# A retention and mixture-of-experts kernel: slot sums in 32-by-32 pieces, phi's products summed in PSUM, out-state in 64-by-64 pieces, phi's loads ahead of routing

## The chip, the cores and the metric

The kernel runs on one core of a Trainium2 chip. The metric is the device time of one execution in microseconds (us). The kernel before was run three times: median 550.13 us, from 546.73 to 552.35. One more execution was profiled; it took 551.17 us, of which the profile's span covers 549.3.

## The reference

Three layers follow one another. All data are float32. The first is a gated retention over 4 batches, 8 heads, 768 steps and head size 64, with a running 64-by-64 state per head:

```python
for t in range(S):
    state = gamma * state + einsum('bhd,bhe->bhde', k[:, :, t], v[:, :, t])
    y[:, :, t] = scale * einsum('bhd,bhde->bhe', q[:, :, t], state)
```

Its output, 3072 tokens of 512 numbers, goes through a top-1 mixture of 8 experts (512 to 1024 to 512, each token through the expert that its gate picks), scaled by the gate's softmax and a sigmoid. The third layer is a soft mixture over 32 slots: `logits = x @ phi`; a softmax over the tokens makes each slot's input `d.T @ x`; 8 more experts act on 4 slots each; a softmax over the slots sends the result back to the tokens:

```python
logits = x @ phi
d = softmax over tokens of logits
slot_input = d.T @ x
slot_out[e] = relu(slot_input[e] @ w1[e]) @ w2[e]
out = softmax over slots of logits @ slot_out
```

## The kernel before, in words

The order of the work is written out by hand on every engine. There are three parts.

**The loop (lines 525 to 552).** 24 tiles of 128 tokens, and two more rounds for what lags. A round follows the table ORDER, whose names are functions: `s0` scores of k with q (line 359, eight products of 64-row halves); `oq` out-state (line 384: four 128-by-128 products of the scaled q with a block-diagonal copy `bds` of the states of two heads, half of it zeros); `os` out-scores (394); `st` the state's update (406, needs `k_scale`'s product of GpSimd, line 342); `xt` transposes (446); gate products and the rank of each token in its expert (427, 439, 493, 494). `pl` (line 508) has GpSimd send the 128 tokens' numbers to their places in a list `inv` in DRAM by an indirect transfer. Those transfers write one tensor, so each waits until the one before has landed, the last one excepted. SyncE's queue issues the loads of tile i+3 (`kt`, `qt`, `vn`, `kn`, 256 KB each), the store `xs` of a finished tile (256 KB), and one load `wt` (512 KB) for phi.

That `wt` load is a quarter of one expert's second weight matrix, transposed. The logits need x times phi where x is h times w2, so the kernel prepares `wps`, w2 times phi, for each expert: `wq_mm` (line 290) multiplies a quarter by phi in four column groups, one for each 128 rows of the contracted axis; ScalarE copies the four partial results (293); `wq_sum` (303) adds them with a product by a selection matrix; ScalarE copies again (307) and after four quarters stores the expert's `wps` (309). There are 32 such units, one for a round of the loop from the fourth on; nine are left behind the loop, and the last five loads (two of them issued before the order is known, three after the first lists) with them.

**Routing (lines 555 to 700).** A product counts the tokens of each expert (`cp`, line 556), VectorE ranks the experts by count, and SyncE and ScalarE read the rank. Then the first weights are loaded (line 191), the first expert's list of tokens (`xidx`, 575, on ScalarE's queue, after the last transfers into `inv`), and a branch is passed on every engine that is taken only when an expert has more tokens than planned. Then GpSimd gathers the tokens' rows (`xg`, 723).

**The experts (lines 890 to 960), then the tail.** For each of 8 experts 8 steps f: TensorE computes `hps` (758) as three products in the rounded float format, ScalarE and VectorE split the weights (200, 201), and beside that `behind(e - 1, f)` does a part of the expert before. At f 2 and 3 the exponentials of the logits are transposed by VectorE into `pd` (823, four 32-row bands), a block-diagonal 128-by-128 matrix for each block of 32 tokens; at f 4 `slot_h` (866) multiplies each of 14, 13 or 12 blocks by the block's `hB` (256 columns), all in one accumulation; at f 5 VectorE transposes the sum (872); at f 6 and 7 `slot_in` (878) multiplies by w2. The tail computes the slots' experts from 128 loads `m` (256 KB each, 52 of them and more prefetched) and writes the output.

## Time and profile before

| what | value |
|---|---|
| median of three runs | 550.13 us |
| the profiled execution | 551.17 us, span 549.3 us |
| TensorE products / weight loads busy | 490.8 us (89%) / 360.2 us (66%) |
| VectorE, ScalarE, GpSimd busy | 266.0, 187.8, 124.5 us |
| read from HBM, written | 118.64 MB, 14.17 MB |

TensorE is busy nearly all the time, but a float32 product shows as two records (two passes), records of different parts of the array overlap, and a record's end is modelled. So the share alone does not tell how much a stage could give; the stages are read one by one. Times in the rows are microseconds from the start of the span.

### The profile page before, as it was taken

To read this page: it belongs to the slowest core of one execution; us is meant where nothing else is said; L and a number is where in the kernel's file an instruction comes from. 1 tells how busy PE (TensorE), PEld (TensorE's weight loads), DVE (VectorE), ACT (ScalarE), POOL (GpSimd) and SP (SyncE) were. 2 spreads that over 40 slices of the span, in tenths; PEclk is the share of its full clock that TensorE was granted. 3 is DMA by queue.
4 is the path that set the end of the run, shared out by engine and by line. 5 is a ranking of instruction groups with operands and counts; after the bars stand their busy time and mean duration, and the time that the engine had idled before them with its cause. 6 is when DMAs were issued, how large, how long until landed. Compare 5 with 4: busy or idle time off the path is not lost.

```text
span 549.3 us, 11022 instructions
## 1 busy us (share of the span) xinstructions
PE 490.8 (89%) x3869; PEld 360.2 (66%) x3869; DVE 266.0 (48%) x820; ACT 187.8 (34%) x486; POOL 124.5 (23%) x130
## 2 busy tenths in 40 slices
PE   4998889997998569999999899999999896789993
PEld 3876667775875348887786877858588582534152
DVE  1756545643663004574554846556475553234032
ACT  1453434452453115442433424233352331013042
POOL 2313222223322112131506023060411103020020
PEclk9999979996996559999999999999999999799997
DMA  8999796979567835782947829387493716999858
GB/s 263 356 335 359 219 340 204 336 237 310 177 207 238 196 114 164 229 260 80 341 153 250 276 73 362 108 297 233 139 333 97 245 58 220 369 388 380 325 184 276
DMA packets 77489, 133.63 MB, mean 243 GB/s; under 512 B 14226, under 2 KB 23056, under 8 KB 77424
## 3 DMA queue, kind: packets, MB, share of 16 engines
q1 hardware_dynamic: 68640, 120.79, 67.0%
q0 software_dynamic: 4176, 8.41, 4.5%
q10 hardware_dynamic: 4608, 3.63, 2.0%
q8 instruction: 33, 0.54, 0.5%
q14 instruction: 32, 0.26, 0.1%
HBM read 118.64 MB, written 14.17 MB: 242 GB/s over the span
## 4 chain that ended last, share of the span: by engine, by line
PE 47%; DMA 6%; DVE 4%; issue 2%; ACT 2%; POOL 1%; SPq 1%; ACTq 1%; POOLq 0%
PE hps L758 19%; PE gps L866 9%; PE slo L878 4%; PE so L1047 4%; PE xps L731 3%; PE fh L1008 3%; DMA w<-in_moe_w_dram 2%; PE lps L789 2%; DVE pd L823 2%; DMA r<-in_moe_w_dram 2%; DMA m<-in_moe_w_dram 1%; PE ops L1105 1%; PE warm L748 1%; ACT ot L1107 1%; POOL xg L723 1%
## 5 line engine op out<-in xcount | busy, mean ns | idle before, releaser
L758 PE MATMUL hps<-xh,wh 128*128 128x416 f32 (+2 forms) x256 | 94.2, 368 | 0.0
L758 PE MATMUL hps<-xh,wl 128*128 128x416 f32 (+2 forms) x256 | 88.8, 347 | 0.0
L758 PE MATMUL hps<-xl,wh 128*128 128x416 f32 (+2 forms) x256 | 88.7, 346 | 0.0
L763 ACT ACTIVATE h<-hps 128x416 f32<-128x416 f32 (+2 forms) x64 | 32.6, 510 | 122.9 <-PE hps L758 112.2
L201 DVE TENSOR_TENSOR wl<-r,wh 128x512 fp32r<-128x512 f32 x64 | 43.6, 682 | 58.8 <-ACT wh L200 57.8
L853 POOL DMA_INDIRECT ctok<-cn,xidx x29 | 28.8, 995 | 185.3 <-DVE cn L850 178.9
L758 PEld LDWEIGHTS hps<-xh,wh 128*128 128x128 f32 x256 | 48.0, 188 | 17.8 <-issue 15.9
L369 DVE TENSOR_TENSOR sS<-s,csa 128x512 f32<-128x512 f32 x48 | 30.9, 685 | 51.8 <-PE s L359 34.5
L866 PE MATMUL gps<-hB,pd 128*128 128x256 f32 x204 | 49.0, 400 | 7.7 <-DVE pd L823 7.4
L866 PEld LDWEIGHTS gps<-hB,pd 128*128 128x128 f32 x204 | 40.1, 200 | 16.2 <-issue 5.8
L758 PEld LDWEIGHTS hps<-xl,wh 128*128 128x128 f32 x256 | 48.1, 188 | 1.6 <-issue 0.8
L508 POOL DMA_INDIRECT inv<-tok,pos x24 | 24.8, 1031 | 106.4 <-DMA inv<-tok,pos 22.4
L758 PEld LDWEIGHTS hps<-xh,wl 128*128 128x128 f32 x256 | 48.1, 188 | 0.8 <-DVE wl L201 0.2
L200 ACT ACTIVATE wh<-r 128x512 fp32r<-128x512 f32 x64 | 40.0, 626 | 15.8 <-DMA r<-in_moe_w_dram 9.6
L723 POOL DMA_INDIRECT xg<-xs,xidx x29 | 29.4, 1015 | 55.9 <-PE xps L731 32.2
L303 PEld LDWEIGHTS wsum<-cs,wr 128*128 128x128 f32 x128 | 22.3, 248 | 22.8 <-issue 10.6
L359 PE MATMUL s<-qt,kt 64*128 64x128 f32 x384 | 31.6, 308 | 5.1 <-DMA qt<-in_qt_dram 5.1
L878 PE MATMUL slo<-w,gt 128*32 128x512 f32 x128 | 30.4, 604 | 4.8 <-DMA w<-in_moe_w_dram 2.2
L770 DVE STREAM_TRANSPOSE hB<-h 128x416 f32<-128x416 f32 (+2 forms) x64 | 34.5, 578 | 0.0
L740 DVE TENSOR_TENSOR xl<-xps,xh 128x416 fp32r<-128x416 f32 (+2 forms) x32 | 18.4, 583 | 28.8 <-issue 20.5
L359 PEld LDWEIGHTS s<-qt,kt 64*128 64x128 f32 x384 | 26.4, 208 | 7.0 <-DMA kt<-in_kt_dram 5.3
L394 PE MATMUL o<-sS,vn 128*64 128x128 f32 x384 | 28.3, 285 | 2.5 <-DVE sS L369 2.5
(144 smaller groups left out, 716.1 us busy)
## 6 DMA issues: line engine op xcount, KB each, us to landing
m<-in_moe_w_dram SPq DMA_DIRECT2D x128, 256.0 KB
wt<-in_moe_w_dram SPq DMA_DIRECT2D x32, 512.0 KB
r<-in_moe_w_dram SPq DMA_DIRECT2D x64, 256.0 KB
w<-in_moe_w_dram SPq DMA_DIRECT2D x64, 256.0 KB
vn<-in_vn_dram SPq DMA_DIRECT2D x24, 256.0 KB
xs<-xnat SPq DMA_DIRECT2D x24, 256.0 KB
kt<-in_kt_dram SPq DMA_DIRECT2D x23, 256.0 KB
qt<-in_qt_dram SPq DMA_DIRECT2D x23, 256.0 KB
```

The lines of the kernel that those rows point to most:

```text
L200: nc.scalar.activation(out=hi, in_=t, func=ACTF.Copy)
L201: nc.vector.tensor_tensor(out=lo, in0=t, in1=hi, op=ALU.subtract)
L359: nc.tensor.matmul(out=ps[h][:, p, :], lhsT=raw["kt", i][r, p, :], rhs=raw["qt", i][r, p, :], start=True, stop=True, tile_position=(64 * h ...
L369: nc.vector.tensor_tensor(out=sS[i][:, :, h, :], in0=sps.pop((i, h)), in1=con("dm", 128).rearrange("p (a b) t -> p a b t", b=2)[:, :, h, : ...
L394: nc.tensor.matmul(out=o[64 * h:64 * h + 64, p, :], lhsT=vv[:, 2 * p + h, :], rhs=s[:, p, h, :], start=(c == 0 and p == 0), stop=True, ski ...
L723: nc.gpsimd.indirect_dma_start(out=xg[e][j][0:r, :], out_offset=None, in_=xs[:, :], in_offset=bass.IndirectOffsetOnAxis(ap=xidx[e][0:r, j: ...
L758: nc.tensor.matmul(out=ps, lhsT=a[:, kk * 128:(kk + 1) * 128], rhs=x[e][kk][:, 0:c], start=(n == 0), stop=(n == 11))
L763: nc.scalar.activation(out=hs[g][:, 0:c], in_=ps, func=ACTF.Relu)
L770: nc.vector.transpose(out=hB[e][:, 0:NB[e], f, :], in_=hs[e * KF + f][:, 0:c].rearrange("p (b t) -> p b t", t=32))
L853: put = nc.gpsimd.indirect_dma_start(out=ctok[:, :], out_offset=bass.IndirectOffsetOnAxis(ap=xidx[e][0:r, j:j + 1], axis=0), in_=cn[0:r, j ...
L866: nc.tensor.matmul(out=ps, lhsT=pd[:, b, :], rhs=hB[e][:, b].rearrange("p f t -> p (f t)"), start=(b == 0), stop=(b == NB[e] - 1))
L878: nc.tensor.matmul(out=slo[e][32 * i:32 * i + 32, :], lhsT=gts[e][:, hf * 4 + i, :], rhs=w2n[e, hf][i], start=(hf == 0), stop=(hf == 1), s ...
```

## The change

Four edits, and the rearrangements that they need.

1. **Slot sums.** `pd` with its zeros is gone; one VectorE transpose over all 128 partitions makes `pT_`. `slot_h` issues, for each block of 32 tokens and each of four 32-row bands, one product of 32 rows by 32 columns (4 times as many products as before, each over 256 columns). The band decides the array's rows and the PSUM bank, the block modulo 4 the array's columns. `slot_c` copies the four banks (two on ScalarE, two on VectorE), and `slot_t` adds the column groups by eight products with the selection matrix.
2. **phi's products.** `wq(e)` takes a whole expert: 16 products, the four column groups each a quarter of the result, accumulated over the contracted axis in PSUM. There is no `wsum` and no copy to it; one VectorE transpose gives the layout that is stored. It runs in rounds 5, 8, ..., 23 of the loop, and once behind it.
3. **Out-state.** Eight products of 64 by 64 in the four quarters of the array; `bds` holds no zeros and is copied by one instruction in place of two. To keep each head in its quarter the order of the heads in x changes, which the host mirrors in the weights' rows.
4. **Loads ahead of routing.** `wt` is loaded at four thirds of a load per round, in contiguous 512 KB, 10 buffers in place of 6; all 32 loads are issued inside the loop. An indirect transfer into `inv` waits for the third before it instead of the one before. The first list `xidx` moves from ScalarE's queue to SyncE's, and the second weight load moves ahead of the later reads of the rank. In ORDER, `st` moves ahead of `os`.

```diff
-ORDER = ("s0 xe sc m0 g1 rm m1 oq gc g2 G0 ne G2 os G3 st G1 G4 G6 rk G7 G8 G9 zk pl G10 "
-         "G5 zq xt G11").split()
+WAT = {5 + 3 * e: e for e in range(E)}
+ORDER = ("s0 xe sc m0 g1 rm m1 oq gc ne g2 G0 G2 wp st os G3 G1 G4 G6 rk G7 G8 G9 zk pl G10 G5 zq xt G11").split()
-PB = dict(s=3, o=1, g=2)
+PB = dict(s=2, o=1, g=2)
...
+        def wq_load(e, kk):
+            if e < E:
+                wtt[e, kk] = wst.tile([128, FF], F32, tag="wt", name="wt")
+                nc.sync.dma_start(out=wtt[e, kk], in_=moe_w2[1, e, kk * 32:(kk + 1) * 32, :].rearrange("a (b f) -> (a b) f", f=FF))
+        def wq(e):
+            ps = pT.tile([128, 512], F32, tag="xn", name="wps")
             for kk in range(KD):
-                nc.tensor.matmul(out=ps[32 * kk:32 * kk + 32, 0:256], lhsT=phi[:, kk, :], rhs=t[:, kk, :],
-                                 start=True, stop=True, skip_group_check=True)
...
+                t = wtt.pop((e, kk))
+                for g in range(4):
+                    nc.tensor.matmul(out=ps[32 * g:32 * g + 32, 0:256], lhsT=phi[:, kk, :], rhs=t[:, 256 * g:256 * g + 256],
+                                     start=(kk == 0), stop=(kk == KD - 1), skip_group_check=True)
+            ws = sc2.tile([128, KF, NS], F32, tag="ws", name="ws")
+            nc.vector.transpose(out=ws, in_=ps[:, 0:256].rearrange("p (b t) -> p b t", t=32))
+            nc.scalar.dma_start(out=wps[e].rearrange("p (f s) -> p f s", s=NS), in_=ws)
...
-                    nc.tensor.matmul(out=o[:, p, :], lhsT=bds[(i - 1) % 2][:, p, :], rhs=q2[i][:, p, :],
-                                     start=(p == 0), stop=False, skip_group_check=True)
+                    for h in range(2):
+                        r = slice(64 * h, 64 * h + 64)
+                        nc.tensor.matmul(out=o_at(i, p, h), lhsT=bds[(i - 1) % 2][r, p, :], rhs=q2[i][r, p, :],
+                                         start=(p < 2), stop=False, tile_position=(64 * h, 64 * (h ^ p % 2)), skip_group_check=True)
...
-            for h in range(2):
-                r = slice(64 * h, 64 * h + 64)
-                nc.scalar.copy(out=bds[i % 2][r, :, r], in_=stp[0][r])
+            nc.scalar.copy(out=bds[i % 2], in_=stp[0])
...
-            if i == NTILE - 1:
-                tc.declare_no_dep(put.ins, places[-1].ins, reason="tokens have distinct slots")
-                after(put, places[-2:-1])
+            for prev in places[-2:]:
+                tc.declare_no_dep(put.ins, prev.ins, reason="tokens have distinct slots")
+            after(put, places[-3:-2])
...
-            wq_load(i + 1)
-            wq_mm(i - WLAG)
-            wq_sum(i - WLAG - 1)
+            for u in range(max(0, (i - 1) * 4 // 3), max(0, i * 4 // 3)):
+                wq_load(*divmod(u, 4))
...
-            after((nc.sync if k else nc.scalar).dma_start(
-                out=xidx[k], in_=inv[bass.ds(er[k] * CAP, 512), :].rearrange("(j p) o -> p (j o)", p=128)), places[-2:])
+            after(nc.sync.dma_start(
+                out=xidx[k], in_=inv[bass.ds(er[k] * CAP, 512), :].rearrange("(j p) o -> p (j o)", p=128)), places[-3:])
...
-            for a in (2 * hf, 2 * hf + 1):
-                q = slice(32 * a, 32 * a + 32)
-                nc.vector.transpose(out=pd[q, 0:NB[e], q], in_=p[q, 0:c].rearrange("p (b t) -> p b t", t=32))
+            nc.vector.transpose(out=pT_[:, 0:NB[e], :], in_=p[:, 0:c].rearrange("p (b t) -> p b t", t=32))
...
-            ps = ps_1.tile([128, KF * 32], F32, tag="g", name="gps")
+            ps = [(ps_x if a < 2 else ps_1).tile([128, KF * 32], F32, tag="xxgo"[a], name="gps") for a in range(4)]
             for b in range(NB[e]):
-                nc.tensor.matmul(out=ps, lhsT=pd[:, b, :], rhs=hB[e][:, b].rearrange("p f t -> p (f t)"),
-                                 start=(b == 0), stop=(b == NB[e] - 1))
+                c = b % 4
+                for a in range(4):
+                    q = slice(32 * a, 32 * a + 32)
+                    nc.tensor.matmul(out=ps[a][32 * c:32 * c + 32, :], lhsT=pT_[q, b, :],
+                                     rhs=hB[e][q, b].rearrange("p f t -> p (f t)"),
+                                     start=(b < 4), stop=(b >= NB[e] - 4), tile_position=(32 * a, 32 * c), skip_group_check=True)
+        def slot_c(e):
+            gsb[e] = sp.tile([128, KF, 4, 32], F32, tag="gsb", name="gsb")
+            for a, ps in enumerate(gps.pop(e)):
+                (nc.vector.tensor_copy if a % 2 else nc.scalar.copy)(out=gsb[e][:, :, a, :], in_=ps.rearrange("p (f t) -> p f t", t=32))
         def slot_t(e):
+            ps = ps_1.tile([128, KF, NS], F32, tag="g", name="gsum")
+            t = gsb.pop(e)
+            for f in range(KF):
+                nc.tensor.matmul(out=ps[:, f, :], lhsT=t[:, f].rearrange("p a t -> p (a t)"), rhs=con("selsum"),
+                                 start=True, stop=True, skip_group_check=True)
             gts[e] = sp.tile([128, KF, NS], F32, tag="gt", name="gt")
-            nc.vector.transpose(out=gts[e], in_=gps.pop(e).rearrange("p (f t) -> p f t", t=32))
+            nc.vector.tensor_copy(out=gts[e], in_=ps)
```

Three places where instructions move. First TensorE in one round of the loop, from out-state on (`o<-q` is out-state, `o<-sS` out-scores, `st` the state, `xn` the transposes, `wps` and `wsum` phi's products). Before, every such round:

```order
L384 MATMUL o<-q_772,bds_140 128x128 x4
L439 MATMUL g<-csa,gsb 128x16
L394 MATMUL o<-sS,vn 64x128 x8
L406 MATMUL st<-vn,k_764 64x64 x8
L446 MATMUL xn<-cs_65,xT 128x128 x4
L290 MATMUL wps<-wt,phi 32x256 x4
L303 MATMUL wsum<-cs,wr 128x32 x2
```

Of the change, a round that has phi's products (every third; the others have the same rows without `wps`):

```order
L378 MATMUL o<-q_867,bds_140 64x128 x8
L431 MATMUL g<-csa,gsb 128x16
L293 MATMUL wps<-wt,phi 32x256 x16
L400 MATMUL st<-vn,k_859 64x64 x8
L388 MATMUL o<-sS,vn 64x128 x8
L438 MATMUL xn<-cs_65,xT 128x128 x4
```

Four unit products and two sums a round became sixteen products every third round, out-state has twice the instructions at half the rows and columns, and the state stands ahead of out-scores.

Second, SyncE's queue from the loop's end to the branch (`ordi` is the rank being read, `r` a load of first weights, `limi` the branch's value). Before:

```order
L281 DMA wt<-in_moe_w_dram 128x1024 x3
L586 TENSOR_LOAD ordi
L586 ISA x2
L191 ISA
L191 DMA r_2572<-in_moe_w_dram 128x512
...
L575 DMA xidx_77<-inv 128x4x1
L281 DMA wt<-in_moe_w_dram 128x1024 x3
L611 TENSOR_LOAD limi
```

Of the change:

```order
L479 DMA xs<-xnat 128x512
L568 TENSOR_LOAD ordi
L568 ISA x2
L196 ISA
L196 DMA r_2491<-in_moe_w_dram 128x512
L564 ISA
L564 DMA xidx_76<-inv 128x4x1
L196 ISA
L196 DMA r_2494<-in_moe_w_dram 128x512
...
L564 DMA xidx_77<-inv 128x4x1
L591 TENSOR_LOAD limi
```

No `wt` load is left between the last store and the branch, and the first list is here.

Third, TensorE at f 4 of an expert with 13 blocks (`hps` the first layer, `gps` the slot sum, `lps` the logits, `gsum` the sum of the column groups). Before:

```order
L758 MATMUL hps<-xl,wh_5060 128x416
L758 MATMUL hps<-xh,wl_5061 128x416
L866 MATMUL gps<-hB,pd 128x256 x13
L789 MATMUL lps<-h,wp 32x416 x4
L758 MATMUL hps<-xh,wh_5087 128x416
```

Of the change:

```order
L738 MATMUL hps<-xh,wl_4965 128x416
L847 MATMUL gps<-hB,pT 32x256 x52
L769 MATMUL lps<-h,wp 32x416 x4
L738 MATMUL hps<-xh,wh_4989 128x416
...
L738 MATMUL hps<-xh,wl_4990 128x416
L862 MATMUL gsum<-cs,gsb 128x32 x8
```

13 products became 52 small ones, and eight more stand one first-layer step later.

## Rows read from the trace of the kernel before

**Rows 1.** The page's first part: busy time, share of the span, instructions.

```profile
PE 490.8 (89%) x3869; PEld 360.2 (66%) x3869; DVE 266.0 (48%) x820; ACT 187.8 (34%) x486; POOL 124.5 (23%) x130
```

**Rows 2.** Windows: stretch and length, busy by engine, granted clock, DMA share, GB/s.

```profile
10.00:30.00 20.00, 19.99 (x270) 17.35 (x270) 12.32 (x53) 7.85 (x26) 5.74 (x5) 1.00 1.02 357
...
13.36:159.33 145.97, 133.56 (x1748) 107.49 (x1747) 85.02 (x373) 62.99 (x206) 40.23 (x39) 0.94 0.89 286
...
172.06:202.07 30.01, 19.25 (x114) 11.15 (x114) 2.87 (x15) 6.12 (x21) 5.99 (x6) 0.50 0.71 189
202.07:462.00 259.93, 253.26 (x1324) 197.16 (x1325) 142.61 (x309) 93.36 (x194) 64.47 (x59) 0.99 0.62 203
462.00:520.00 58.00, 49.05 (x343) 20.73 (x339) 18.29 (x65) 7.37 (x19) 2.99 (x3) 0.94 1.01 367
```

**Rows 3.** Windows of three single rounds, from scores to scores.

```profile
18.88:23.67 4.79, 4.79 (x74) 4.21 (x73) 3.55 (x16) 2.27 (x8) 0.84 (x1) 1.00 1.05 397
...
97.32:103.24 5.92, 5.92 (x86) 4.89 (x85) 3.49 (x17) 3.04 (x10) 2.06 (x2) 1.00 1.05 371
...
54.13:62.50 8.37, 6.37 (x86) 4.93 (x85) 4.58 (x17) 3.15 (x10) 2.06 (x2) 1.00 0.67 144
```

**Rows 4.** Timeline of TensorE in the round at 97.32: start, length, what, records.

```profile
97.32 1.16 PE L359 MATMUL s<-qt,kt 64*128 64x128 f32 x16
...
98.83 1.14 PE L384 MATMUL o<-q,bds 128*128 128x128 f32 x8
...
100.96 0.63 PE L406 MATMUL st<-vn,k 128*64 128x64 f32 x16
...
102.11 0.64 PE L290 MATMUL wps<-wt,phi 128*32 128x256 f32 x8
102.68 0.63 PE L303 MATMUL wsum<-cs,wr 128*128 128x32 f32 x4
```

**Rows 5.** Timeline of GpSimd, 40 to 62: in brackets idle time, and what ended it.

```profile
41.48 0.98 POOL L508 DMA_INDIRECT inv<-tok,pos  x1 [7.46 <-DMA inv<-tok,pos]
...
49.65 1.01 POOL L508 DMA_INDIRECT inv<-tok,pos  x1 [6.11 <-PE g L439]
```

**Rows 6.** Timeline of TensorE, 48 to 62: the state's update.

```profile
51.80 0.69 PE L406 MATMUL st<-vn,k 128*64 128x64 f32 x16 [1.31 <-POOL k L342]
```

**Rows 7.** Timeline of all engines from the loop's end to the experts' start.

```profile
167.49 0.98 POOL L508 DMA_INDIRECT inv<-tok,pos  x1 [4.22 <-DMA inv<-tok,pos]
...
174.40 0.98 POOL L508 DMA_INDIRECT inv<-tok,pos  x1 [0.30 <-issue]
...
175.21 3.19 SPq L191 DMA_DIRECT2D r<-in_moe_w_dram  x3
...
183.16 0.41 ACTq L575 DMA_DIRECT2D xidx<-inv  x1
...
189.57 1.07 POOL L723 DMA_INDIRECT xg<-xs,xidx  x1 [14.19 <-DMA wt<-in_moe_w_dram]
...
197.28 0.34 ACTq L309 DMA_DIRECT2D wps<-ws  x1
...
201.39 0.63 ACT L200 ACTIVATE wh<-r 128x512 fp32r<-128x512 f32 x1 [4.14 <-ACTq L700]
...
202.07 3.77 PE L748 MATMUL warm<-wh 128*128 128x512 f32 x8 [5.07 <-ACT wh L200]
```

**Rows 8.** Groups by line: busy us, mean ns of one; idle before, what ended it.

```profile
L866 PE MATMUL gps<-hB,pd 128*128 128x256 f32 x204 | 49.0, 400 | 7.7 <-DVE pd L823 7.4
...
L823 DVE STREAM_TRANSPOSE pd<-lm 32x416 f32<-32x416 f32 (+2 forms) x32 | 19.0, 595 | 7.5 <-ACT lm L815 7.0
```

**Rows 9.** The chain of work that ended last: start, length, what.

```profile
256.91 1.00 PE slo L878 x8
...
278.13 5.82 PE gps L866 x26
...
514.02 6.72 DMA m<-in_moe_w_dram
```

More of the change, by code (lines that the diff above doesn't have):

```diff
@@ L94, in _consts, with _rows @@
     return np.concatenate(cols, 1), off, ni, na, nb
+def _rows():
+    return np.concatenate([64 * (2 * p + (h ^ (p & 1))) + np.arange(64) for p in range(H // 2) for h in range(2)])
 def _layout(inputs):
@@ L314, in retention_moe_kernel @@
+        bds = [one.tile([128, 4, D], F32, name=f"bds{i}") for i in range(2)]
         run = one.tile([128, NTILE + 1, E], BF16, name="run")
@@ L715, in retention_moe_kernel @@
         ps_1 = pb.enter_context(tc.tile_pool(name="ps_1", bufs=1, space=PSUM))
[L717 removed]
+        xg, xh, xl, hs, hB, wp, w2n, lps, lrs, lrs2, sms, msks, lms, ces, gps, gsb, gts, slo = ({} for _ in range(18))
         puts = {}
```

102 lines of the change are left out of this document (31 added, 71 removed).

## The prediction, made before the changed kernel had run

> **What bounds the kernel now.** I read the page's first part, then windows by stage, then TensorE's and GpSimd's timelines inside the loop, the timeline of all engines around routing, and the groups and the chain of waits for the experts. TensorE is busy 89% of the span [rows 1], but that hides four stages with four limits [rows 2].
>
> The loop runs 22 rounds in 145.97 us, 6.63 us each. A round in which nothing is late takes 5.92 us, all of it TensorE (the window at 97.32 [rows 3]). The rest are stalls: the round at 54.13 takes 8.37 us with TensorE busy for 6.37, and DMA at 144 GB/s, so neither is the limit there. GpSimd is: one transfer into `inv` waits 7.46 us for the one before to land, the next leaves 8.17 us after it [rows 5], the product k that stands behind it in GpSimd's queue is late, and TensorE's state update waits 1.31 us for k [rows 6]. With DMA full (share about 1) the queues move 357 GB/s [rows 2].
>
> Routing takes 172.06 to 202.07 at a granted clock of 0.50, the lower of the two levels, 1.2 GHz [rows 2]. The last transfer into `inv` leaves at 174.40, the list is fetched at 183.16, the gathers start at 189.57; ScalarE serves phi's left-over products until 197.28, passes the branch and starts at 201.39; TensorE's warm-up products then run from 202.07 for 3.77 us [rows 7]. The experts are bound by TensorE: 253.26 busy of 259.93 [rows 2]; the slot sums lie on the chain, 5.82 us for 26 records [rows 9]. The tail is bound by DMA: 367 GB/s from 462 to 520 [rows 2], with a last wait of 6.72 us for m [rows 9].
>
> **The loop.** From the free round of 5.92 us go `wsum` (102.68 to the next round at 103.24: 0.56) and the unit `wps` (102.11 to 102.68: 0.57) [rows 3, 4]. Sixteen products each third round cost at most four units, 2.28 us, or 0.76 a round. Out-state has the same columns in twice as many products, with four parts of the array in place of one: if they overlap in full it halves, so of 1.14 us [rows 4] 0.57 go; bounds 0 and 0.57, and I take the full saving, since the scores already overlap halves of rows: 16 records of 128 columns would take 1.79 us one by one (half of the 0.224 us that 256 columns take [rows 9], times 16) and take 1.16 [rows 4]. TensorE's price is 5.92 - 0.56 - 0.57 + 0.76 - 0.57 = 4.98 us. DMA is then the higher one: five transfers of 262,144 bytes and four thirds of 524,288 are 2.01 MB a round, at 357 GB/s 5.63 us. The transfers into `inv` now wait for the third before: at 8.17 us for one landing that allows one every 2.7 us, no limit. The loop becomes 22 x 5.63 = 124 us: **22 us less**. Ends: 36 less (TensorE's price alone), 10 less (6.2 us a round, stalls half kept). ScalarE's and VectorE's part (one state copy in place of two, two copies fewer a unit, one transpose more an expert) is hidden: they are busy 3.04 and 3.49 of 5.92 [rows 3]. `wq` shares the bank of the transposes, so that these wait for VectorE's transpose; `st` and `os` lie between, 0.63 and more [rows 4]. `st` ahead of `os` costs a wait if k is late again, with `os` queued behind it.
>
> **Routing.** The wait that ends last is ScalarE's, for phi's products; one expert's sixteen are left in place of nine units. Next late are the gathers. The rank is known 3.15 us after 172.06, when the weight load leaves (175.21). The last transfer into `inv` no longer waits for its predecessors. In the calm stretch GpSimd stood 4.22 us until one had landed, after 0.98 us of issue [rows 7]; its place is computed before `cp`, so I let it leave 1 us ahead of the window's start, and it lands at about +4.0, so the list is fetched at +4.3 in place of +11.1. From there to the first gather I keep the 6.41 us of before (183.16 to 189.57). Four gathers at some 1.35 us are 5.4, and I take 4.2 for the last to land, as a transfer into `inv` does. TensorE gets its data at 4.3 + 6.4 + 5.4 + 4.2 = +20.3; before, the warm-up ended at 202.07 + 3.77, +33.8. **13.5 us less.** ScalarE is ready long before that (four units, a store, 4.14 us of branch). Ends: 6.7 less if the list isn't fetched earlier (17.5 + 5.4 + 4.2 = 27.1), 20 less if fetch and landing take half. SyncE has the list's wait ahead of the second weight load now: harmless, since the first expert step needs the gathers, too.
>
> **The experts.** Seven slot sums lie between first-layer steps, with 90 blocks: before, 180 records at 0.224 us (5.82 / 26) are 40.3 us. After, there are 720 records of 256 columns. With all 16 pieces at once they go in 26 rounds of 16 products, two passes each: 26 x 2 x 0.224 = 11.6 us. Each also needs `slot_t`: 16 records with 128-column weights, as in `wsum` (0.56 / 4 = 0.14 us): 7 x 16 x 0.14 = 15.7 us. Together 27.3, 13.0 less. Bounds for the 720 records: 11.6 us, and 161 us if none overlaps. I take the lower end, as the nearest rows are the column groups: eight records of 512 columns, 3.6 us one by one, take 1.00 us [rows 9]. Three of four transposes of 0.595 us go; TensorE waited 7.4 us on them [rows 8], some of it in the last expert; I count 2. **15 us less.** The four copies stand beside the logits and a first-layer step. DMA has room (share 0.62 [rows 2]).
>
> As a check from the Trainium skill, "TensorE: Matmul & The Clock Gate", "Part 3: Packing small matmuls — row/col tiling": 16 such pieces were measured 10.6 times as fast as one after another. By that the 720 records would be an estimate of 161 / 10.6 = 15 us, 4 us more than mine. No row here shows 16 pieces.
>
> **The tail: nothing.** The last expert's slot sum has only 1.6 us or so of DMA pauses around it; the loads for m set the end [rows 2, 9]. If that cover were gone, some 3 us would come back.
>
> Sum against the profiled execution: 551.2 - 22 - 13.5 - 15 = 500.7. It stands 1 us above the median of the runs shown, so **500 us** for the median.
>
> **Rivals.**
>
> *Pieces leave TensorE at a fixed pace.* The densest round has 74 products with their weight loads in 4.79 us, 64.7 ns each [rows 3]; against a pace speak the 16 records of `st` in 0.63 us, 39 ns each [rows 4], though so few may have been queued ahead. At 64.7 ns the slot sums take 720 x 0.0647 = 46.6, with `slot_t` 62.3: 22 us more, 20 after the transposes. The round has 92.7 records, 6.0 us: the loop gains 14. Total 551.2 - 14 - 13.5 + 20 = 543.7. A pace half way, 40 ns, gives 518. The Trainium skill, same page, section "Wait — 56ns, not 53.3ns?", has such a rule: decoded in ucode, a matmul takes the sequencer about 62 ns, which binds once the array's work is shorter. By it the slot sums would be an estimate of 44.6 us. The trace doesn't decide.
>
> *The loop keeps part of its stalls.* Loads, the store in SyncE's order and TensorE alternate in being late; 6.2 us a round, 10 us less in place of 22: 513. For it: full-DMA rounds reach 371 and 397 GB/s [rows 3], but the mean is 286 [rows 2]. Against: the stalls seen lead back to GpSimd.
>
> *Slower: row bands don't run together.* `slot_h` issues its four row bands innermost, all in one column group; rows show four column groups at once, but only two row parts. With two at a time 720 x 0.112 = 80.6 us, with `slot_t` 96.3: 56 more, 54 after the transposes, and 551.2 - 22 - 13.5 + 54 = 570. It decides from 86 ns a record: (40.3 - 15.7 + 2 + 35.5) / 720. Against it: the two parts of the scores overlap though they share all columns.
>
> **Chances and numbers.** My forecast, 488 to 512: 0.60. The stalled loop, 512 to 520: 0.15. The half-way pace, about 518: 0.05. The full pace, 544: 0.12. Slower, 570: 0.05. Better than 488: 0.03. The range 484 to 530 leaves out the full pace, the slower case and most of what lies below 488, about 0.19. About 1% (5.5 us) is what a measurement of this kernel can tell from no change: faster by more 0.92, within it 0.03, slower 0.05.
>
> **What would show it.** Window of the loop: 22 rounds in about 124 us, DMA share near 1, no GpSimd wait for `inv` above 3 us. From `cp` to the first transposes about 20 us. The group `gps` some 12 to 15 us busy over seven experts, `gsum` near 2.2 us each. The tail unchanged from the end of the experts. I am wrong if `gps` records start 40 ns apart or more in the middle of a burst, if the loop stays above 6 us a round with DMA below a share of 0.9, or if ScalarE or the branch, not the gathers, ends the routing.

## The result, and the profile after

The changed kernel takes 527.03 us (median of four runs, 521.83 to 531.60), beside 548.43 for the kernel before in the same call: ratio 0.9569, 95% interval 0.9458 to 0.9681. The forecast was 500 in a range of 484 to 530. So the sign was right, the time lies at the range's upper end, and less than half of the forecast 50 us came. The profiled execution took 524.94 us, its span 523.2 in place of 549.3.

The page's first part, which answers to [rows 1]:

```profile
PE 457.1 (87%) x4641; PEld 322.9 (62%) x4641; DVE 248.8 (48%) x818; ACT 168.1 (32%) x418; POOL 130.0 (25%) x129
```

TensorE has 34 us less work in more instructions, but the span fell by 26: some of what was taken from TensorE came back as waiting. Windows of the changed kernel, with the columns of [rows 2]: the loop from the scores of tile 1 to those of tile 23; routing from `cp` to the first first-layer step; from there to the last such step; and a wider window of the end.

```profile
12.18:158.67 146.49, 124.26 (x1856) 92.57 (x1855) 78.68 (x378) 47.03 (x151) 47.45 (x40) 0.90 0.96 306
167.99:194.01 26.02, 12.29 (x57) 6.07 (x56) 5.63 (x23) 2.95 (x5) 6.31 (x7) 0.54 0.55 140
194.01:431.94 237.93, 234.53 (x1938) 182.59 (x1938) 131.06 (x299) 95.58 (x204) 61.45 (x57) 0.99 0.66 215
437.50:523.20 85.70, 68.46 (x614) 31.10 (x614) 26.04 (x84) 17.06 (x43) 7.39 (x11) 0.89 0.90 322
```

The same two middle stretches in the kernel before:

```profile
172.06:208.35 36.29, 25.52 (x139) 15.60 (x139) 4.79 (x17) 7.75 (x24) 6.06 (x7) 0.54 0.62 166
208.35:457.08 248.73, 243.13 (x1286) 191.90 (x1286) 140.68 (x306) 91.24 (x190) 62.21 (x58) 1.00 0.62 205
```

The account of the 26.1 us: the 22 rounds of the loop 146.49 against 145.97 [rows 2], nothing gained; the stretch from tile 23 to `cp` 9.32 against 12.73, 3.4 less; routing 10.3 less; the experts 10.8 less; all else (start and tail) 2.2 less. Routing and experts behaved nearly as forecast. The loop did not.

What a round of the loop looks like now: windows of one undisturbed round, and of one with `wq` in it.

```profile
29.45:34.04 4.59, 4.59 (x82) 3.71 (x81) 3.91 (x19) 2.21 (x8) 1.05 (x2) 1.00 1.04 258
55.15:68.75 13.60, 8.73 (x114) 5.50 (x113) 4.22 (x20) 2.11 (x8) 3.39 (x3) 0.75 1.03 282
```

Two rounds of three have no `wq`, and most of these take 4.6 us, all TensorE, where before an undisturbed one took 5.92 [rows 3]: the work was taken out. Every third, the one with `wq`, takes 10.5 to 13.6. Its timeline, with SyncE's queue (SPq) and ScalarE's (ACTq) from the earlier such round on:

```profile
43.01 0.36 ACTq L297 DMA_DIRECT2D wps<-ws  x1
...
44.67 0.33 SPq L479 DMA_DIRECT2D xs<-xnat  x1
48.91 0.33 SPq L285 DMA_DIRECT2D wt<-in_moe_w_dram  x1
...
57.66 1.07 PE L293 MATMUL wps<-wt,phi 128*32 128x256 f32 x16
...
63.02 1.08 PE L293 MATMUL wps<-wt,phi 128*32 128x256 f32 x8 [4.29 <-DMA wt<-in_moe_w_dram]
64.68 1.08 PE L293 MATMUL wps<-wt,phi 128*32 128x256 f32 x8 [0.57 <-DMA wt<-in_moe_w_dram]
```

TensorE stands in `wq` for a piece of `wt`, with everything else of the round queued behind it. The piece is late because SyncE issued nothing from 44.67 to 48.91. The profile's list of waits says for what (engine, line, released by: us in all, times, longest; 12.18 to 158.67):

```profile
SPq L479 <- DMA xs<-xnat: 12.7, 6, 4.9
SPq L285 <- DMA wps<-ws: 12.5, 3, 5.5
...
SPq L315 <- DMA wps<-ws: 10.1, 2, 5.8
...
SPq L479 <- DMA wps<-ws: 4.1, 1, 4.1
```

The three rows behind `wps` are 26.7 us, one hold for each of the six stores in these rounds. The longest single row, `xs` behind the `xs` of an earlier round, is not what lengthens the loop: in e2 below it is down to 1.3 us, and the loop is as long.

A load of `wt` reads nothing that the store of `wps` writes. The link shows in the compiled order of the changed kernel, where each row names the semaphores that it waits on. On SyncE's queue:

```
52 L315 DMA kn<-in_kn_dram 128x512 [waits DMAHW4_49,Pool_49]
53 L479 DMA xs<-xnat 128x512 [waits DMAHW6_49,Activation_49]
...
59 L479 DMA xs<-xnat 128x512 [waits DMAHW4_49,Activation_49]
60 L285 DMA wt<-in_moe_w_dram 128x1024 [waits DMAHW5_49]
```

and on ScalarE's queue:

```
31 L297 DMA wps<-ws 128x256 [waits DMAHW5_49,DVE_49]
```

In this compiled program SyncE's and ScalarE's transfers share eight semaphores, DMAHW0 to 7, which go round in the order of the program; each transfer waits until the one eight turns ahead of it has landed. ScalarE's store takes turn 5 between SyncE's rows 52 and 53, so SyncE's row 60, the `wt` load at 48.91, waits until a store has landed that itself had to wait for `wq`. `wq` waits for `wt`, the store for `wq`, the next `wt` for the store. Behind each of the six stores SyncE's next transfer leaves 5.9 to 6.8 us after the store was issued (48.91 after 43.01 here), so what SyncE stands for is the store's landing. Then the transfers run dry: 78 GB/s from 48.91 to 52.00, where nothing new had been queued in time.

```profile
48.91:52.00 3.09, 3.09 (x54) 2.44 (x50) 2.21 (x15) 1.35 (x5) 1.65 (x2) 1.00 0.65 78
```

The kernel before had such waits, too (13 us, two of 6.5). There the puts were late as well: TensorE's state update waited for k in five of its rounds. Both in the list of waits of before's loop:

```profile
SPq L329 <- DMA wps<-ws: 6.5, 1, 6.5
SPq L281 <- DMA wps<-ws: 6.5, 1, 6.5
```

```profile
PE st L406 <- POOL k L342: 9.9, 5, 3.0
```

In the changed kernel no row of the loop has `st` waiting for k, as [rows 6] had, nor a put waiting for the one before, as [rows 5] had. One wait was removed and another stands in its place.

### The profile page after: what moved, and what is told of

Read it like the earlier page. It is cut to its first block, busy times and chain, and to the rows that moved or that the text cites. A ratio compares the mean times of both kernels' runs of the same rounds, so it can differ in the third digit from the quotient of the medians.

```text
span 523.2 us, 12481 instructions
## 1 busy us (share of the span) xinstructions
PE 457.1 (87%) x4641; PEld 322.9 (62%) x4641; DVE 248.8 (48%) x818; ACT 168.1 (32%) x418; POOL 130.0 (25%) x129
## 4 chain that ended last, share of the span: by engine, by line
PE 56%; DMA 33%; DVE 3%; issue 2%; ACT 2%; SPq 2%; another core or an unknown queue 1%; ACTq 1%; POOLq 0%; POOL 0%
PE hps L738 26%; DMA inv<-tok,pos 9%; DMA wt<-in_moe_w_dram 7%; PE slo L871 5%; PE gps L847 4%; PE so L1040 3%; PE fh L1001 3%; PE gsum L862 3%; PE xps L711 3%; DMA xs<-xnat 3%; DMA vn<-in_vn_dram 3%; DMA w<-in_moe_w_dram 2%; PE lps L769 2%; DMA qt<-in_qt_dram 2%; DMA xg<-xs,xidx 1%
## 5 line engine op out<-in xcount | busy, mean ns | idle before, releaser
L738 PE MATMUL hps<-xh,wh 128*128 128x416 f32 (+2 forms) x256 | 95.5, 373 | 0.0
L500 POOL DMA_INDIRECT inv<-tok,pos x24 | 31.7, 1321 | 83.2 <-DVE run L460 71.6
L293 PE MATMUL wps<-wt,phi 128*32 128x256 f32 x256 | 21.0, 433 | 23.6 <-DMA wt<-in_moe_w_dram 22.8
L871 PE MATMUL slo<-w,gt 128*32 128x512 f32 x128 | 32.1, 656 | 4.5 <-DMA w<-in_moe_w_dram 2.2
L388 PE MATMUL o<-sS,vn 128*64 128x128 f32 x384 | 32.0, 321 | 0.0
L328 POOL TENSOR_TENSOR k<-kn,cs 128x512 f32<-128x512 f32 x20 | 20.9, 1044 | 32.5 <-DMA kn<-in_kn_dram 31.1
L388 PEld LDWEIGHTS o<-sS,vn 128*64 128x64 f32 x384 | 26.4, 166 | 2.4 <-issue 2.4
```

The lines of the kernel that those rows point to most:

```text
L388: nc.tensor.matmul(out=o_at(i, p, h), lhsT=vv[:, 2 * p + h, :], rhs=s[:, p, h, :], start=(c == 0 and p < 2), stop=True, skip_group_check=True)
L500: put = nc.gpsimd.indirect_dma_start(out=inv[:, :], out_offset=bass.IndirectOffsetOnAxis(ap=pos[:, i:i + 1], axis=0), in_=tok[:, i:i + 1], ...
L738: nc.tensor.matmul(out=ps, lhsT=a[:, kk * 128:(kk + 1) * 128], rhs=x[e][kk][:, 0:c], start=(n == 0), stop=(n == 11))
L871: nc.tensor.matmul(out=slo[e][32 * i:32 * i + 32, :], lhsT=gts[e][:, hf * 4 + i, :], rhs=w2n[e, hf][i], start=(hf == 0), stop=(hf == 1), s ...
```

## The experiments

"Queue" is the theory above. Its rivals were "bytes" (the transfers can't bring 2.01 MB a round faster) and "lead" (`wq` is asked for too soon behind its loads). Ratios are to the kernel before, run in the same call; before took 548.1, 560.2, 545.9 and 560.6 us in the four calls, so medians are only compared inside a call, and ratios between calls. The expectations in us counted from the times of the first calls; in a call where before took 560 us, the ratio is what to read them by.

**e1: the stores behind the loop.**

```diff
-            ws = sc2.tile([128, KF, NS], F32, tag="ws", name="ws")
+            ws = sc2.tile([128, KF, NS], F32, tag="ws", name="ws", bufs=E)
...
+            wss[e] = ws
             nc.vector.transpose(out=ws, in_=ps[:, 0:256].rearrange("p (b t) -> p b t", t=32))
-            nc.scalar.dma_start(out=wps[e].rearrange("p (f s) -> p f s", s=NS), in_=ws)
+
+        def wq_store(e):
+            nc.scalar.dma_start(out=wps[e].rearrange("p (f s) -> p f s", s=NS), in_=wss.pop(e))
...
+        for e in range(E):
+            wq_store(e)
```

> The changed kernel with one thing moved: the seven stores of phi's products (wps) leave the loop and are issued after it, so each product stays in SBUF (a buffer per expert) until then. Theory 'queue': in the changed kernel SyncE issues its transfers by eight semaphores in turn, a store on ScalarE's queue takes one turn, and the eighth transfer behind it may not be issued until that store has landed; SyncE sat idle 26.7 us of the loop's 146.5 behind wps stores, and TensorE's wq then waits for wt (23 us). By it the 22 rounds fall from 146.5 to 120 to 127 us and the time from 527 to 502 to 510. Rival 'bytes': 2.01 MB a round at the 320 GB/s that the transfers reach while they run is the bound; the loop stays at 142 to 147 us and the time at 523 to 530. Rival 'lead': wq asks for its last piece only about one and a half rounds behind the issue of its load; the loop stays above 140 us too.

Measured: 513.62 us, ratio 0.9327 (0.9254 to 0.9399). No `wps` wait is left in SyncE's loop. The loop took 134.55 us: 12 less, which is more than both rivals allow and less than the theory's 20 to 27. TensorE still waited for `wt`. SyncE's issues now stood still for more than 2.5 us four times, 11 us in all, in place of nine times and 38.5.

```profile
12.19:146.74 134.55, 116.66 (x1856) 87.59 (x1855) 79.03 (x378) 47.12 (x151) 46.81 (x40) 0.95 1.03 321
```

**e2: `wq` two rounds later, and e3: both edits.**

```diff
-WAT = {5 + 3 * e: e for e in range(E)}
+WAT = {7 + 3 * e: e for e in range(E)}
```

> The changed kernel with WAT = 7 + 3e in place of 5 + 3e: each expert's products are taken two rounds later behind the same loads, the stores stay in the loop. Theory 'queue': TensorE no longer waits for wt, so the store is issued sooner in its round, but the eighth transfer behind it still waits for it: loop 130 to 140 us, time 511 to 521. Rival 'lead': all of the wait goes, loop 118 to 126 us, time 500 to 508. Rival 'bytes': loop 142 to 147 us, time 523 to 530.

> Both edits: stores behind the loop, and WAT = 7 + 3e. 'Queue' and 'lead' together: the loop falls to TensorE's round or the transfers' (4.7 to 5.4 us), 104 to 119 us, time 486 to 502. 'Bytes': 2.01 MB at 320 GB/s is 6.2 us a round, 137 us and more, time 518 or more.

Measured: e2 526.05 us, 0.9565 (0.9486 to 0.9643), the same as the changed kernel. That misses the theory's 511 to 521 and lies where "bytes" had it; its loop took 148.74, where the theory had 130 to 140. But the wait changed its name: TensorE no longer waits in `wq`; its scores wait for `qt`, which SyncE issues late behind the store's turn. SyncE stood for 28.6 us behind `wps` (the first row below, and one of 7.0): so the hold does not need the wait in `wq`, only a store that lands late. e3: 508.47 us, 0.9284 (0.9222 to 0.9346), with e8 below the best version here.

e2's waits in the loop:

```profile
SPq L285 <- DMA wps<-ws: 21.6, 3, 8.1
...
PE s L345 <- DMA qt<-in_qt_dram: 18.4, 5, 4.5
```

e3's loop:

```profile
12.18:139.41 127.23, 114.44 (x1856) 86.79 (x1854) 82.28 (x378) 47.26 (x151) 44.02 (x40) 0.96 1.03 341
```

Lead by itself is worth nothing while the turn stands; with the turn gone it is worth 7 us of loop. e3 missed its expected 486 to 502: its rounds take 5.78 us, more than the 5.2 that TensorE is busy in one (114.44 / 22), at a DMA share of 1.03. So "bytes" has a part, though not the 518 us and more that it forecast.

**e4 and e5: half of phi's bytes**, in the changed kernel and in e3. Half of each piece of `wt` is left out and the other half used twice.

```diff
-                nc.sync.dma_start(out=wtt[e, kk], in_=moe_w2[1, e, kk * 32:(kk + 1) * 32, :].rearrange("a (b f) -> (a b) f", f=FF))
+                nc.sync.dma_start(out=wtt[e, kk][:, 0:512], in_=moe_w2[1, e, kk * 32:(kk + 1) * 32, :].rearrange("a (b f) -> (a b) f", f=FF)[:, 0:512])
...
-                    nc.tensor.matmul(out=ps[32 * g:32 * g + 32, 0:256], lhsT=phi[:, kk, :], rhs=t[:, 256 * g:256 * g + 256],
+                    nc.tensor.matmul(out=ps[32 * g:32 * g + 32, 0:256], lhsT=phi[:, kk, :], rhs=t[:, 256 * (g % 2):256 * (g % 2) + 256],
```

> The changed kernel with half of each wt tile loaded (columns 0 to 511) and used twice, so TensorE's work and all waits stay and phi's loads bring 256 KB in place of 512: half of phi's products are wrong by that. Theory 'bytes': 1.67 MB a round at 320 GB/s is 5.2 us, loop 113 to 122 us, time 495 to 503. Theory 'queue': the store still holds SyncE's turn, the wait for wt gets shorter by what the smaller transfer saves: loop 128 to 138 us, time 510 to 519. 'Lead': a smaller transfer lands sooner, loop 125 to 135 us, time 508 to 516.

> Stores behind the loop and WAT = 7 + 3e as in e3_both, and half of each wt tile loaded and used twice as in e4_half_bytes (half of phi's products are wrong by that). Where the store's turn and phi's bytes together are what holds the loop, both gone leave TensorE's own round (4.6 us in e3_both's undisturbed rounds): 22 rounds in 101 to 112 us, time 482 to 493. Rival: something else in SyncE's order (the xs store behind ScalarE's xnat) still holds it, loop 118 us and more, time 498 or more.

Measured: e4 507.93 us, 0.9267 (0.9193 to 0.9340); loop 132.78. e5 0.9062 (0.8993 to 0.9131), loop 127.83, where 101 to 112 was expected. e4's loop is where "queue" (128 to 138) and "lead" (125 to 135) had it, and not where "bytes" did (113 to 122); its time lies just below the 510 and 508 that these two began at. That smaller transfers land sooner and so shorten the circle would explain it; it was not shown. e5 says that phi's bytes are not all that is left: against e3's ratio it gains 0.022, 12 us for 7.7 MB fewer, and its loop stays far from TensorE's price, where the rival (118 us and more) had it.

```profile
12.33:140.16 127.83, 114.74 (x1857) 87.39 (x1855) 81.01 (x378) 47.06 (x151) 43.17 (x40) 0.96 1.02 286
```

The DMA share is 1.02 here at 286 GB/s and 1.03 in e3 at 341: a full share is no full rate. Halving `wt` halved its packets (from 4,096 to 2,048 bytes) and left their number: 20,686 packets in e5's loop, 20,518 in e3's. A packet of 2,048 bytes has the same median in both, 84 ns, but a mean of 115 ns in e5 and 96 in e3 (104 in e8, of e5's call). The share adds up the time that packets take, however long each of them takes.

**e6: the slot sums of before in the changed kernel.** `p_tr`, `slot_h`, `slot_t` and the tile `pd` are those of before, `slot_c` goes.

```diff
-                for a in range(4):
-                    q = slice(32 * a, 32 * a + 32)
-                    nc.tensor.matmul(out=ps[a][32 * c:32 * c + 32, :], lhsT=pT_[q, b, :],
-                                     rhs=hB[e][q, b].rearrange("p f t -> p (f t)"),
-                                     start=(b < 4), stop=(b >= NB[e] - 4), tile_position=(32 * a, 32 * c), skip_group_check=True)
+                nc.tensor.matmul(out=ps, lhsT=pd[:, b, :], rhs=hB[e][:, b].rearrange("p f t -> p (f t)"),
+                                 start=(b == 0), stop=(b == NB[e] - 1))
```

> The changed kernel with the slot sums of before (one 128-by-128 product a block with the weights on a block diagonal, two transposes a half, no second summation), everything else as changed. The changed kernel spends 28.5 us on gps and gsum of seven experts, before spent 40.3 on gps: on TensorE's path that is 11.8 us for seven and some 1 to 2 for the last, so the time rises from 527 to 537 to 542. Rival: the experts are held by something else and the new sums were hidden, time 524 to 530.

Measured: 547.89 us, 0.9772 (0.9713 to 0.9832), 0.0203 over the changed kernel, 11 us (10 to 15 were expected). The stage shows it directly: the experts' stretch takes 249.62 us in place of 237.93, as long as before's 248.73. The slot sums are worth 11.7 us.

```profile
12.22:171.96 159.74, 124.11 (x1856) 90.08 (x1855) 79.42 (x378) 46.91 (x151) 46.71 (x40) 0.89 0.95 278
...
207.95:457.57 249.62, 246.01 (x1286) 193.63 (x1286) 140.15 (x306) 90.70 (x190) 62.23 (x58) 0.99 0.61 204
```

(Its loop, the changed kernel's word for word, took 159.74 us in this call, 13 more than in the first: TensorE's work is the same 124, the transfers ran at 278 GB/s in place of 306.)

**e7: e3 with one put at a time, and e8: the store by GpSimd's queue**, which takes none of the eight turns (with WAT = 7 + 3e).

```diff
-            for prev in places[-2:]:
-                tc.declare_no_dep(put.ins, prev.ins, reason="tokens have distinct slots")
-            after(put, places[-3:-2])
+            if i == NTILE - 1:
+                tc.declare_no_dep(put.ins, places[-1].ins, reason="tokens have distinct slots")
+                after(put, places[-2:-1])
```

```diff
-            nc.scalar.dma_start(out=wps[e].rearrange("p (f s) -> p f s", s=NS), in_=ws)
+            nc.gpsimd.dma_start(out=wps[e].rearrange("p (f s) -> p f s", s=NS), in_=ws)
```

> e3_both (508.5 us) with the puts one at a time again, as in the kernel before. Theory 'queue and bytes': the loop's rounds are now 5.8 us by the transfers, and a put at a time costs nothing until rounds get shorter than its landing: time 505 to 512. Rival: the put still sets the pace where the transfers don't, as the prediction had it (1 to 1.3 us in a round in which POOL's k is late): 515 to 530.

> The changed kernel with WAT = 7 + 3e, and each wps store issued in its place in the loop, but on GpSimd's queue in place of ScalarE's, so it takes none of the eight turns that SyncE's transfers go by. Theory 'queue': what cost in e2_wq_later (526 us) was the turn alone, so this is as good as e3_both: loop 124 to 131 us, time 504 to 512. Rival: the store's own traffic or its place costs: time 518 to 528.

Measured: e7 538.22 us, 0.9628 (0.9577 to 0.9678): 18.6 us more than e8 in the same call. My expectation (nothing) fell and the rival, the prediction's own view of the puts, holds: `st` waits for k again. Of the 18.6 us, 13.9 are in the loop. e8: 519.67 us, 0.9280 (0.9232 to 0.9329), equal to e3's ratio; in us it missed the expected 504 to 512, in a call where before took 12 us longer. The store stays in the loop with all its bytes, and with WAT = 7 + 3e, which by itself was worth nothing (e2), only its turn is gone: the loop takes 140.25 us, where the changed kernel's took 159.74 in the same call (e6). That is the plainest evidence for "queue". One rival is left by the runs alone: e1, e3 and e8 also free ScalarE, whose order stands at the store until `wq` is transposed. The waits of the changed kernel's loop speak against it: of those of TensorE's products, 19.9 us are for `wt` and 0.7 for ScalarE, and of SyncE's under 4 us are for ScalarE.

e7's loop, and e8's:

```profile
11.89:166.02 154.13, 122.59 (x1857) 95.16 (x1855) 82.60 (x378) 46.83 (x151) 40.70 (x39) 0.88 0.93 286
```

```profile
12.11:152.36 140.25, 122.21 (x1857) 92.38 (x1855) 82.30 (x378) 47.43 (x151) 46.74 (x46) 0.90 1.02 318
```

```profile
PE st L403 <- POOL k L331: 28.3, 7, 5.9
```

**e9 and e10: 256 KB more a round, stored or loaded**, both on e8.

```diff
             nc.sync.dma_start(out=xs[i * 128:(i + 1) * 128, :], in_=t)
+            nc.sync.dma_start(out=xs2[i * 128:(i + 1) * 128, :], in_=t)
```

```diff
             nc.sync.dma_start(out=xs[i * 128:(i + 1) * 128, :], in_=t)
+            again = sc2.tile([128, DM], F32, tag="again", name="again")
+            nc.sync.dma_start(out=again, in_=kt[i])
```

> e8_pool_store with each tile's 256 KB of xs stored a second time, to a buffer that nothing reads. e8_pool_store's ratio to before is 0.928. If the transfers' bytes now set the loop's rounds, 22 times 0.262 MB at 341 GB/s (the rate in e3_both's loop) adds 17 us, 0.031 in the ratio (0.955 to 0.965); if it is the writes that hold up the other packets, it adds more than the same bytes of loads do, 25 us or more (0.975 and up); if nothing but latency and turns holds the loop, under 8 us (below 0.943).

> e8_pool_store with 256 KB loaded once more a round in place of e9_extra_store's second store (kt's tile into a buffer that nothing reads), at the same place of SyncE's order. Bytes as the bound: 17 us as in e9_extra_store (0.955 to 0.965). Writes as the trouble: less than e9_extra_store by 8 us or more.

Measured: e9 526.19 us, 0.9658 (0.9610 to 0.9706); e10 524.25 us, 0.9601 (0.9553 to 0.9649). Against e8's 0.9280 that is 0.038 and 0.032, 21 and 18 us for 5.8 MB: 280 and 330 GB/s. Once the turn is gone, a further 256 KB a round costs its time at about the rate that the loop reaches, and stores cost no more than loads within the noise. Each also takes a turn more, and bytes and turns are not told apart here: e5, which took bytes away and no transfer, gained 12 us for 7.7 MB.

**e11: the kernel before with its store on GpSimd's queue.**

```diff
-                nc.scalar.dma_start(out=wps[e], in_=wsum.pop(e))
+                nc.gpsimd.dma_start(out=wps[e], in_=wsum.pop(e))
```

> The kernel before with one word changed: its wps stores (four in the loop) go by GpSimd's queue in place of ScalarE's. SyncE sat idle 13 us of before's loop behind two of the stores. Theory 'queue': before was held by the store's turn too, and gains 6 to 13 us: ratio 0.975 to 0.99. Rival: before's loop is held by its puts, and GpSimd gets more to do: 0.995 to 1.02.

Measured: 556.57 us, 1.0233 (1.0162 to 1.0304), slower. The theory's expectation failed here, and the rival's 0.995 to 1.02 was passed. The loop took 145.46 us, within 1 us of before's 145.97, so the 13 us behind `wps` look not to have been on before's path (the two loops are from two calls). The loss lies behind the loop: 44.28 us from `cp` on in place of 36.29. A store queued on GpSimd stands in the way of puts there: GpSimd waited 12.5 us for the last sums, with the last puts behind them.

```profile
POOL wps L309 <- ACT ws L307: 12.5, 1, 12.5
```

**v1, v3b and v4: versions.** v3b issues e8's stores a round later, behind the put (a step `ws` in ORDER). v1 and v4 take three experts' products out of the loop; in v1 the late stores go by ScalarE's queue, in v4 (on v3b) the last loads stand ahead of the expert order and the late stores go by SyncE's.

```diff
-WAT = {7 + 3 * e: e for e in range(E)}
+WAT = {7 + 4 * e: e for e in range(5)}
...
-            for u in range(max(0, (i - 1) * 4 // 3), max(0, i * 4 // 3)):
+            for u in range(max(0, i - 1), max(0, i)):
```

> A version that takes the theory further: stores on GpSimd's queue as in e8_pool_store, and phi's products for five experts in the loop (a load a round, products every fourth round) and for three behind it, where TensorE stands idle for some 20 us of routing and the transfers run at 140 GB/s. Loop: 1.83 MB a round in place of 2.01, 9% of 127 us, 8 to 13 us less; routing: three products of 3.4 us and 6.3 MB beside the gathers, 0 to 8 us more. Ratio 0.905 to 0.93 (e8_pool_store 0.928). Rival: the late loads delay the gathers by as much as the loop gives: 0.93 to 0.945.

> e8_pool_store with each store issued a round later, behind the next round's put, so GpSimd doesn't stand waiting for the transpose (9 us in e8_pool_store's loop) and k isn't late by it. Ratio to before 0.918 to 0.930 (e8_pool_store 0.928): GpSimd's wait was mostly beside the transfers. Rival: that wait was on the path, 0.905 to 0.915.

> v3b with phi's products for five experts in the loop and three behind it, mended against v1_five_in_loop (0.952), where ScalarE's queue stood behind the late stores and the gathers behind that, 51.5 us from cp to hps in place of 25 to 28: now the last loads are issued ahead of the expert order, and the late stores go by SyncE's queue behind the index loads. Theory 'bytes': the loop ends 17 to 21 us earlier, as in v1_five_in_loop, and routing takes 26 to 34 us: ratio 0.885 to 0.915. Rival: the 3.7 MB behind the loop hold the index loads and the gathers up by what the loop gives: 0.92 to 0.94.

Measured: v1 519.03 us, 0.9518 (0.9469 to 0.9566); v3b 522.15, 0.9313 (0.9239 to 0.9387); v4 520.10, 0.9295 (0.9227 to 0.9364). v3b is e8 again. v1 and v4 missed the ratios that they were made for (0.93 and 0.915 at most). v1's loop is the shortest, 119.64 us, and all of it is lost in routing, 51.52; v4's, 13.2 us shorter than v3b's, is lost to 40.70 there. Stretch of routing in v4, and what ScalarE waited for in it:

```profile
151.00:191.70 40.70, 21.89 (x125) 8.33 (x123) 6.55 (x24) 2.95 (x5) 6.61 (x8) 0.50 0.70 211
```

```profile
ACT wh L205 <- ACTq L694: 25.9, 1, 25.9
```

L694 is the branch for overflowing experts; GpSimd's first gather, behind the same branch, came after 27.3 us of standing idle. The trace says what they stood for. The branch's value `limi` is worked out on VectorE, and there it stands behind the transposes of the late products, which wait for the late `wt`:

```profile
172.73 0.45 DVE L296 STREAM_TRANSPOSE ws<-wps 128x256 f32<-128x256 f32 x1 [4.70 <-PE wps L293]
...
173.48 0.16 DVE L604 CAST limi<-lim 1x9 int32<-1x9 f32 x1
```

The cast ends at 173.64; the semaphore waits ahead of the branch, in which ScalarE had stood since 151.38 and GpSimd since 151.85, both end at 173.68. In v1 the cast ends at 174.68 and GpSimd's wait at 174.72. So it is neither SyncE nor a store, but late products ahead of `limi` in VectorE's order. No version that works out `limi` first was run.

**e12 and e13: the put edit by itself**: undone in the changed kernel (e7's edit), and made alone in the kernel before (e7's edit turned round).

> The changed kernel with the puts one at a time again. If its loop was held by the store's turn whatever the puts do, nothing changes: ratio 0.95 to 0.965 (changed kernel 0.957). If puts and turns add up, as e7_one_put against e3_both (0.9628 against 0.9284) would have it, 0.98 to 0.995.

> The kernel before with three puts in flight, and nothing else. The prediction's view: puts held some 6 of before's rounds by 1 to 3 us, 10 to 15 us in all, ratio 0.972 to 0.982. Rival: before's rounds are held by the transfers and the stores' turns as the changed kernel's are, and waits only change their name: 0.99 to 1.005.

Measured: e13 539.14 us, 0.9614 (0.9535 to 0.9692): this edit alone brings 3.9%, about as much as the whole change, and more than the 1.8 to 2.8% expected. e12 540.06 us, 0.9651 (0.9582 to 0.9719): undoing it in the changed kernel costs 0.008, within the intervals, although its puts and `st` wait again. Where the transfers' circle holds the loop, the puts' waits stand beside it.

e12's waits in the loop:

```profile
POOL inv L500 <- DMA inv<-tok,pos: 31.0, 6, 6.6
...
PE st L400 <- POOL k L328: 21.4, 8, 6.8
```

## Why the prediction came out as it did

**The loop: the failed step.** It was "DMA is then the higher one: ... at 357 GB/s 5.63 us. ... The loop becomes 22 x 5.63 = 124 us: 22 us less". It took for granted that the transfers are always queued. In fact they ran at 306 GB/s over the loop, and the move of phi's products made a circle: one store in three rounds, behind sixteen products that wait for loads, holds one of eight turns that the loads go by. It cost 12 us alone (e1), 19 with the lead (e3: 127.23 us, 5.78 a round, 3% over my 5.63), and e8 shows that it is the turn and not the store's bytes. The prediction's own sign of being wrong, over 6 us a round at a DMA share below 0.9, came true by half: the share was 0.96, which told nothing of the rate. The prediction's rival "The loop keeps part of its stalls" named the store in SyncE's order and gave it 0.15; it had 6.2 us a round, and 6.66 came. So the rival's mechanism was right in kind, too small in size, and traced to the wrong store: I looked at `xs` in SyncE's own queue and not at `wps` in ScalarE's. The list of SyncE's waits of before, with 13 us behind `wps`, shows the tie, but not its price: by e11 those 13 us were hardly on before's path.

The other parts of that step came out in part. TensorE's price was put at 4.98 us, with `wq` spread over three rounds; two rounds of 4.59 and one with `wq` of 6.45 (from e3, below) are 5.2 a round. So it was a little too low, but still under the transfers' 5.63. Out-state takes 0.67 us in place of 1.14 (0.57 was forecast).

```profile
80.91:87.36 6.45, 6.45 (x113) 4.64 (x112) 4.75 (x20) 1.90 (x8) 2.84 (x3) 1.00 1.02 329
```

The puts did hold the kernel before: e13 brings 21 us. (In e3 they would cost 18.6, by e7.) Of the forecast's 22 us some 15.6 were such stalls (22 rounds of 6.63 in place of 5.92), so the puts were worth more than it said. In the changed kernel the turn took that away: without the put edit it is only 0.008 slower (e12).

**Routing: a quarter too large, and one step right by luck.** 13.5 us were forecast, 10.3 came, and the gathers end it as said. The timeline from `cp` at 167.99 answers to [rows 7]:

```profile
169.22 0.98 POOL L500 DMA_INDIRECT inv<-tok,pos  x1 [0.31 <-DVE sq L551]
...
171.51 0.35 SPq L196 DMA_DIRECT2D r<-in_moe_w_dram  x1
...
175.13 0.45 DVE L296 STREAM_TRANSPOSE ws<-wps 128x256 f32<-128x256 f32 x1 [4.31 <-PE wps L293]
...
175.88 0.16 DVE L590 CAST limi<-lim 1x9 int32<-1x9 f32 x1
...
177.18 0.40 SPq L564 DMA_DIRECT2D xidx<-inv  x1
...
180.89 0.63 ACT L205 ACTIVATE wh<-r 128x512 fp32r<-128x512 f32 x1 [12.05 <-ACTq L680]
...
182.93 1.07 POOL L703 DMA_INDIRECT xg<-xs,xidx  x1 [12.73 <-DMA r<-in_moe_w_dram]
...
186.92 0.95 POOL L703 DMA_INDIRECT xg<-xs,xidx  x1 [0.30 <-issue]
...
190.33 3.76 PE L711 MATMUL xps<-cs,xg 64*128 64x64 f32 x13 [0.46 <-DMA xg<-xs,xidx]
```

The list is fetched at +9.2 and not at +4.3: the last put left at +1.2, not 1 us ahead of `cp`, and took 8.0 us to the fetch, as the 8.17 between puts in the loop had it, and not 5. From the fetch to the first gather it was 5.8 us (6.4 said), but by another path: the list had landed at 180.58, and GpSimd asked for it only at 181.95, since it had passed the branch first. The branch's value stands behind the last transpose of phi's products in VectorE's order (175.13 and 175.88; GpSimd's wait for it ended at 176.08), as in v1 and v4. Before, the list had landed last, at 188.71, and the first gather left at 189.57. The prediction priced the branch on ScalarE alone. The last of four gathers left 4.0 later and landed in 3.4 (5.4 and 4.2 said). TensorE has its data at +22.3; +20.3 was forecast.

**The experts: right, 3 to 4 us too large.** 15 were forecast, the stretch is 10.8 shorter, and e6 gives 11.7. Two steps of the chain of waits, which answers to [rows 9]; then the two groups, which answer to [rows 8]:

```profile
264.46 2.49 PE gps L847 x93
...
270.23 1.71 PE gsum L862 x16
```

```profile
L847 PE MATMUL gps<-hB,pT 32*32 32x256 f32 x816 | 20.1, 402 | 3.4 <-DVE pT L801 3.4
...
L862 PE MATMUL gsum<-cs,gsb 128*128 128x32 f32 x128 | 16.7, 287 | 0.9 <-DVE gsb L855 0.9
```

Over the seven, `gps` takes 16.6 us of the chain where I had 11.6, and `gsum` 11.9 where I had 15.7; the sum, 28.5, is near my 27.3. 720 records in 16.6 us are 23 ns each: with 16 pieces at once the row bands run together, which refutes both the slower rival (from 86 ns on) and the fixed pace of 64.7. The Trainium skill, "TensorE: Matmul & The Clock Gate", section "Wait — 56ns, not 53.3ns?", gives about 62 ns for a matmul that is decoded in ucode; at 23 ns a record that rule does not bind here, and no run shows how these are decoded. The 10.6-fold speed-up in "Part 3: Packing small matmuls — row/col tiling" of the same page of the Trainium skill gave an estimate of 15 us, and the trace agrees better with that than with my full overlap. The 2 us for transposes didn't come.

**The tail: nothing, as said.** The last expert's `gps` and `gsum` take longer than the others', and the end is still set by a wait for m, in the chain of waits:

```profile
442.37 3.02 PE gps L847 x94
446.28 3.61 PE gsum L862 x16
...
488.47 5.41 DMA m<-in_moe_w_dram
```

**The sum.** Forecast -22, -13.5, -15 and 0; measured in the profiles: +0.5 in the loop and -3.4 behind it, -10.3, -10.8, and -2.2 at the start and the tail. Of the 24 us that are missing, 22.5 are the 22 rounds and 7.4 the routing and the experts; 5.6 came unforecast elsewhere. e3 gives 18.6 us back (527.0 to 508.5).

What stays open: why packets of the same size take longer on average in e5's loop than in e3's, so that fewer bytes bring no shorter loop; and whether bytes or turns set the price of e9 and e10.

## What to carry to other kernels

Transfers from different engines can be tied to each other by nothing but their turn at a shared set of semaphores: before moving a store that waits for late work, count which loads stand eight transfers behind it, and read the waits of the issuing engine, not only those of the computing ones. Such a wait need not be on the path (e11). A wait's price has to be asked of the kernel in which it will stand: the same put edit was worth 21 us in one kernel and 0.008 of the time, within the noise, in the next, since there something else was late at the same time. Work moved out of a stretch bound by transfers is only gained if the place that it goes to has no branch or queue that everything must pass: look for what the branch's value waits for.

## What the runs showed of the hardware

A DMA share of 1 told little of the rate: 258 GB/s in one round at 1.04, 286 in e5 at 1.02, 341 in e3 at 1.03, and 397 in a round of before at 1.05 [rows 3]. The forecast's 357 was the rate of one calm stretch. The same loop took 146.5 us in one call and 159.7 in another (e6), with TensorE's 124 us unchanged and the transfers at 306 and 278 GB/s. The granted clock was below 1.00 (2.4 GHz) in each of the six rounds in which TensorE waited for `wt`, 0.75 to 0.87 over the round, and 1.00 in most others. The loss outlasts the wait: the scores at 45.34, 4 us behind the end of one, took 2.08 us in place of 1.16 (below). TensorE was busy for 124.26 us in the changed kernel's loop and for 114.44 in e3's, with the same 1856 records, at 0.90 and 0.96. So some 10 of the 19 us between the two loops are not idle time but the same work, done at the lower clock.

```profile
45.34 2.08 PE L345 MATMUL s<-qt,kt 64*128 64x128 f32 x16
...
55.15 1.16 PE L345 MATMUL s<-qt,kt 64*128 64x128 f32 x16
```
